# Cross-covariance attention with a highway layer: small loads moved to SyncE's queue, one more chunk of norms off TensorE, loads kept away from DMA transposes

## The chip, the cores and the metric

The kernel runs on one core of a Trainium2 chip. The core has TensorE (PE, matrix products), VectorE (DVE), ScalarE (ACT), GpSimd (POOL) and SyncE (SP), which work side by side and wait for each other by semaphores, and 16 DMA engines that carry out the transfers which any of them issues. The metric is the device time of one execution in microseconds; before the change the median of three runs was 268.25 us (268.19 to 269.06). The profile is of one more execution, with a span of 267.1 us from the first instruction of the program to the last.

## The reference, cut to what matters

```python
# attention; q, k, v: (4, 6336, 256) f32, tau = 1
qn = q / (norm(q, axis=1) + 1e-6)              # norms of columns, over the 6336 rows
kn = k / (norm(k, axis=1) + 1e-6)
a  = softmax(kn.transpose(0, 2, 1) @ qn / tau)  # one 256 x 256 matrix per batch
x  = (v @ a).reshape(25344, 256)
# highway layer
H  = maximum(x @ w_h, 0)
T  = sigmoid(x @ w_t + b_t)
out = T * H + (1 - T) * x                       # (25344, 256) f32
```

All of q and k of a batch has to be summed up before the first row of that batch's output can be computed.

## The kernel before, in words

*Tiling.* A batch has 6336 rows: 48 rows on each of 128 partitions, in six chunks of eight (0.5 MB each as f16, 1 MB read as f32), and a rest of 192 rows (96 partitions by 2, chunk 6). There are 25 pairs of rows a batch; pairs are numbered through, `g` from 0 to 99, so batch 3 is 75 to 99.

*Stage 1* (`stage1`, line 360) has 50 steps a batch, `s0.0` to `s3.49`. One step adds k^T q to two PSUM banks (line 372) and, for the norms, k^T k (line 374) and q^T q (line 376), of which only the diagonals are used. For the first `OFF[nm][b]` chunks (line 26: five of q in batches 1 to 3) the sums of squares are made elsewhere: ACT squares half a chunk (line 397, `sqq`), GpSimd adds it to an accumulator (line 403, `adq`), then folds it (`fsq`), and one product adds it over the partitions. The products of line 376 are left out for these chunks.

*The chain* of a batch (`plan_chain`, line 485; names `c0.` to `c3.`) takes diagonals, roots on GpSimd (line 513), scaling, exponential, transposes, the fold of the softmax with the weights of the highway layer (`fold`, line 619, which needs both weights), and leaves three 256 x 256 matrices in f16.

*Stage 2* works on pairs. v is transposed (`tr`, line 673) and moved out of PSUM (`ev`), and then come three groups of four products (line 728, names `h`, `t`, `x`), a preset of the bias by ACT or DVE (`b`, line 481 or 483), relu and gate on ACT (`r`, `g`, lines 785 and 804), and two operations on DVE (`p`, `y`, lines 815 and 861). Stage 2 of a batch is interleaved with stage 1 of the next.  For chunks 3 to 6 of batch 3 (`BY_DMA`, line 23), the transpose of v is a DMA instead (`T3.3` to `T3.6`, line 696), issued by SyncE.

*Loads and stores.* GpSimd issues all loads (`load`, line 251) as transfers that cast f32 to f16 on the way: q, k, v by chunks, and the rests of q and k of batch 0 (line 256), the weights (`load_w`, line 233, names `Lw0`, `Lw1`) and the bias row (`load_b`, line 238, `Lb0`, `Lb1`). In batch 0 the steps run over chunks 0 to 2, then the rest, then chunks 3 to 5 (`order_of`, line 350). SyncE issues stores (`O`, line 870), holds (`H`, line 904: tiny transfers that read a row of a later output buffer, and so keep the stores behind them on the queue until that chunk has been begun) and the DMA transposes, strictly in order.

*The order of all work* is the text `ORDER` (lines 36 to 112), written out by hand or by a planner outside the kernel: `Plan.run` (line 147) goes through it and emits each task; each engine executes its own tasks in that order. `/ACT` or `/DVE` after a name chooses the engine. Buffers are rings: q and k have five chunks each, v five, output chunks seven; a load waits until the users of the chunk five loads earlier are done.

Of the kernel before, what the change touches and what calls it, by code (L numbers as in the profile page):

```python
# [15 lines left out]
P = 128  # L16
# [9 lines left out]
OFF = {"q": (0, 5, 5, 5), "k": (0, 0, 0, 0)}  # L26
# [10 lines left out]
Lk0.0 Lk0.1 Lq0.0 Lk0.6 const Lq0.1 Lk0.2 Lq0.2 Lb1 Lq0.6 Lb0 Lq0.3 s0.0 Lk0.3 s0.1 s0.2 s0.3 Lq0.4.0 s0.4  # L37
s0.5 s0.6 s0.7 s0.8 Lq0.4.4 s0.9 s0.10 s0.11 s0.12 s0.13 Lk0.4.0 s0.14 s0.15 Lk0.4.4 s0.16 Lk0.5.0 s0.17
Lq0.5.0 s0.18 s0.19 s0.20 Lk0.5.4 s0.21 spt s0.22 ball s0.23 s0.48 s0.49 Lq0.5.4 s0.24 s0.25 s0.26 Lk0.5.6
s0.27 s0.28 s0.29 Lq0.5.6 s0.30 s0.31 Lk1.0.0 s0.32 s0.33 s0.34 Lq1.0.0 s0.35 s0.36 s0.37 Lw1 s0.38 spd1 s0.39  # L40
Lw0 s0.40 s0.41 Lv0.0 s0.42 Lq1.0.4 s0.43 s0.44 s0.45 s0.46 s0.47 spd0 c0.dq0 c0.g0/ACT b0/ACT c0.dq1 c0.dk0
c0.nq c0.dk1 sqq1.0.0 s1.0 c0.nk c0.iq c0.b c0.g1/ACT Lk1.0.4 c0.ik s1.1 Lv0.1 s1.2 c0.s0 s1.3 Lq1.1 c0.s1
c0.e0 Lk1.1 c0.e1 c0.tr0 c0.r0 Lv0.2 c0.v0/ACT c0.tr1 c0.r1 Lq1.2 c0.f0 c0.v1/ACT c0.a0 Lk1.2 tr0 c0.h0/DVE
c0.f1 ev0/ACT c0.t0/ACT tr2 c0.t1/DVE c0.a1 t0 ev2/ACT c0.h1/ACT tr1 g0 h0 ev1/DVE b1/DVE tr3 r0 h1 ev3/ACT t1
r1 x0 g1 s1.4 p0 tr5 b2/ACT x1 ev5/DVE sqq1.0.1 t2 y0 s1.5 p1 s1.6 g2 adq1.0.1 h2 b3/ACT y1 tr4 s1.7 r2 t3
ev4/DVE h3 g3 tr6 x2 r3 Lv0.3 b4/DVE ev6/ACT Lq1.3 p2 sqq1.1.0 s1.8 s1.9 y2 t4 adq1.1.0 x3 g4 s1.10 p3 tr7
b5/ACT s1.11 ev7/DVE s1.12 sqq1.1.1 t5 y3 h4 Lk1.3 g5 h5 Lk1.4 r4 tr8 s1.13 Lq1.4 b6/ACT ev8/DVE x4 Lv0.4 r5
tr9 t6 p4 Lk1.6 ev9/ACT s1.14 g6 tr10 y4 s1.15 b7/ACT x5 h6 ev10/ACT p5 Lq1.5 t7 r6 s1.16 adq1.1.1 y5 g7 tr11
x6 ev11/DVE b8/ACT h7 p6 s1.17 r7 t8 y6 s1.18 g8 s1.19 h8 sqq1.2.0 b9/DVE tr12 x7 ev12/DVE r8 s1.20 adq1.2.0
p7 t9 sqq1.2.1 s1.21 y7 tr14 x8 g9 s1.22 p8 b10/ACT h9 adq1.2.1 s1.23 ev14/ACT y8 r9 t10 s1.24 g10 tr15 s1.25  # L50
sqq1.3.0 b11/DVE s1.26 h10 t11 ev15/ACT adq1.3.0 s1.27 g11 x9 tr13 b12/ACT s1.28 p9 s1.29 r10 ev13/DVE s1.30
t12 y9 Lq1.6 x10 Lk1.5 g12 h11 p10 Lv0.5 s1.31 r11 s1.32 Lq2.0 y10 s1.33 b13/ACT Lk2.0 x11 sqq1.3.1 t13 Lv1.0
p11 s1.34 g13 h12 adq1.3.1 y11 tr17 r12 s1.35 ev17/DVE s1.36 sqq1.4.0 b14/DVE x12 h13 p12 tr16 t14 adq1.4.0
ev16/ACT y12 s1.37 r13 s1.38 g14 x13 sqq1.4.1 h14 b15/DVE tr18 s1.39 p13 Lq2.1 r14 t15 Lq2.2 y13 x14 g15
adq1.4.1 s1.40 b16/DVE h15 s1.41 ev18/DVE r15 p14 t16 s1.42 g16 y14 x15 Lv0.6 tr20 b17/ACT s1.43 Lk2.1 p15 t17
Lv1.3 ev20/DVE h16 y15 fsq1.0 g17 s1.44 r16 h17 b18/DVE tr21 r17 x16 fsq1.1 ev21/DVE t18 p16 tr19 x17 g18
ev19/DVE s1.45 y16 b19/ACT s1.46 p17 t19 s1.47 y17 g19 s1.48 sqq2.0.0 b20/DVE s1.49 tr22 c1.dq0 h18 ev22/ACT
c1.dk1 h19 c1.g1/ACT c1.dk0 r18 opq1 c1.dq1 r19 t20 kpq1 c1.rq c1.g0/ACT x18 c1.nq g20 tr23 s2.0 p18 ev23/ACT
Lv1.1 x19 b21/ACT c1.iq tr25 Lk2.2 s2.1 y18 ev25/ACT t21 Lv1.2 sqq2.0.1 s2.2 p19 c1.nk tr26 h20 g21 ev26/DVE
adq2.0.1 s2.3 y19 r20 s2.4 tr27 b22/ACT c1.ik x20 sqq2.1.0 ev27/DVE h21 p20 tr24 t22 r21 ev24/DVE adq2.1.0  # L60
s2.5 y20 g22 tr28 x21 ev28/ACT H5 h22 b23/ACT p21 O0.0.0 s2.6 r22 c1.b y21 sqq2.1.1 s2.7 Lq2.3 x22 c1.s0 Lk2.3
h23 c1.s1 c1.e0 p22 t23 adq2.1.1 c1.e1 c1.tr0 c1.r0 s2.8 r23 s2.9 c1.r1 g23 c1.tr1 x23 c1.v0/DVE b24/ACT y22
s2.10 s2.11 Lq2.6 c1.v1/ACT p23 t24 sqq2.2.0 Lk2.4 tr29 c1.f1 y23 Lq2.4 s2.12 c1.h1/DVE c1.t1/ACT Lv1.4 c1.f0
g24 ev29/DVE h24 adq2.2.0 c1.t0/ACT b25/DVE s2.13 r24 s2.14 t25 c1.h0/ACT c1.a1 x24 c1.a0 h25 g25 p24 s2.15
r25 s2.16 y24 s2.17 sqq2.2.1 tr30 b26/DVE x25 h26 adq2.2.1 p25 t26 r26 s2.18 y25 g26 s2.19 x26 ev30/DVE
b27/ACT H6 h27 p26 O0.1.0 t27 r27 tr32 O0.2.0 y26 s2.20 g27 x27 O0.3.0 ev32/DVE b28/ACT h28 p27 tr31 r28 t28
ev31/DVE s2.21 y27 g28 tr33 s2.22 ev33/ACT b29/DVE x28 sqq2.3.0 h29 p28 t29 r29 adq2.3.0 s2.23 y28 s2.24 g29
x29 b30/ACT h30 p29 tr34 r30 t30 y29 s2.25 Lq2.5 g30 x30 Lv1.5 sqq2.3.1 h31 b31/DVE Lk2.5 s2.26 p30 s2.27 r31
adq2.3.1 t31 ev34/DVE s2.28 y30 g31 tr35 x31 ev35/DVE b32/ACT h32 p31 tr36 r32 t32 Lq3.0 y31 s2.29 g32 Lv1.6
x32 ev36/ACT h33 p32 b33/ACT tr37 s2.30 r33 ev37/DVE t33 y32 x33 g33 tr38 h34 ev38/DVE b34/ACT s2.31 p33 r34  # L70
tr40 t34 ev40/ACT y33 s2.32 g34 tr39 x34 H8 ev39/DVE b35/ACT h35 H7 p34 tr41 r35 t35 y34 s2.33 g35 x35
ev41/DVE sqq2.4.0 h36 b36/DVE tr42 s2.34 p35 ev42/ACT t36 adq2.4.0 r36 tr43 y35 s2.35 g36 x36 sqq2.4.1 b37/DVE
h37 s2.36 p36 t37 r37 Lk2.6 ev43/DVE s2.37 g37 y36 Lk3.0 s2.38 x37 adq2.4.1 b38/ACT h39 p37 tr44 r39 t38
ev44/DVE s2.39 y37 g38 tr45 x39 ev45/ACT b39/DVE h38 Lv2.0 tr46 fsq2.0 r38 t39 s2.40 g39 x38 fsq2.1 s2.41 p39
b40/ACT s2.42 ev46/ACT Lk3.1 y39 t40 Lq3.1 tr47 p38 h40 g40 Lq3.3 s2.43 y38 r40 Lv2.1 s2.44 sqq3.0.0 ev47/DVE
x40 b41/DVE h41 p40 tr48 r41 t41 s2.45 y40 g41 x41 ev48/DVE h42 b42/ACT p41 tr49 r42 t42 y41 s2.46 g42 s2.47
H10 ev49/ACT b43/DVE h43 sqq3.0.1 O0.4.0 x42 t43 O0.6 r43 p42 tr50 s2.48 g43 y42 s2.49 ev50/ACT x43 b44/ACT
c2.dq0 tr51 c2.g1/ACT c2.dk0 t44 c2.g0/ACT c2.dq1 h44 ev51/ACT c2.dk1 g44 opq2 p43 c2.nk b45/ACT s3.0 kpq2
s3.1 c2.rq r44 y43 t45 c2.nq tr53 s3.2 g45 Lk3.2 ev53/DVE x44 c2.ik Lq3.2 b46/ACT h45 c2.iq Lv2.2 tr52 t46 p44
ev52/ACT Lk3.3 s3.3 r45 c2.b Lk3.4 y44 g46 s3.4 Lq3.4 x45 b47/ACT c2.s0 adq3.0.1 s3.5 c2.s1 c2.e0 t47 p45  # L80
c2.e1 c2.tr0 c2.r0 s3.6 g47 c2.tr1 s3.7 c2.v0/ACT c2.v1/DVE s3.8 b48/ACT y45 c2.f0 Lv2.3 s3.9 H11 c2.h0/DVE
c2.t0/ACT c2.f1 c2.r1 O0.5.0 h46 Lq3.5 c2.h1/DVE s3.10 O1.0.0 r46 t48 O1.1.0 c2.t1/ACT tr54 x46 ev54/ACT h47
g48 p46 s3.11 r47 Lk3.5 tr55 b49/DVE s3.12 c2.a0 x47 y46 ev55/ACT t49 sqq3.1.0 p47 h48 s3.13 r48 adq3.1.0 y47
s3.14 tr56 g49 x48 ev56/ACT h49 b50/DVE s3.15 p48 r49 t50 c2.a1 s3.16 Lv2.4 y48 g50 x49 s3.17 b51/ACT p49 h50
# [1032 lines left out]
```

## Time and profile before

| what | before |
|---|---|
| time, median of 3 | 268.25 us |
| span of the profile | 267.1 us |
| TensorE / ACT / DVE / GpSimd busy | 91% / 74% / 69% / 48% |
| first product of stage 1 | 11.5 us |
| DMA moved (f16 counted where f16 is written) | 67.2 MB; HBM read 78.4 MB, written 26.0 MB |
| products of line 376 in the trace (128 partitions) | 144, 217 ns long each, start to start 0.055 us |
| squares of half a chunk on ACT, line 397 | 27, 1056 ns each |
| additions on GpSimd, line 403 | 27, 2371 ns each |

Matrix products are pipelined: one of 256 columns is 272 ns long, but the next starts 0.11 us after it, so a sum of lengths overstates TensorE's work. A line with a wait reads: engine and line that waited, for whom, microseconds in total, times, longest. GB/s counts what is written, so a stretch of loads (f32 read, f16 written) that keeps all DMA engines busy shows some 210 GB/s and a stretch of stores some 400.

### The profile page before, as it was taken

The page shows a single profiled execution, that of the slowest core. Times are in us where ns is not written, and L with a number is a line of the kernel's source. Part 1 is how long each engine was busy: PE and PEld are TensorE (multiplying, and loading weights), DVE is VectorE, ACT ScalarE, POOL GpSimd, SP SyncE. Part 2 cuts the span into 40 slices and gives each one's busy share as a digit, 9 for nine tenths or more (in the row PEclk, how much of TensorE's full clock was granted, in tenths as well). Part 3 has the DMA queues.
Part 4 walks back from the last instruction along what each step waited for, and adds up shares of the span by engine and source line. Part 5 has one row for each costly group of instructions (what it writes and reads, how often), then busy time and mean ns, then how long its engine had stood idle before and what let it go on. Part 6 is the DMA issues. An engine that isn't in the chain of part 4 may idle for free.

```text
span 267.1 us, 6250 instructions
## 1 busy us (share of the span) xinstructions
PE 243.9 (91%) x2438; PEld 216.4 (81%) x2438; DVE 183.4 (69%) x380; ACT 198.7 (74%) x378; POOL 127.4 (48%) x143
## 2 busy tenths in 40 slices
PE   0298988999999999999999999999999999999980
PEld 0297975899999998899999988999989888888870
DVE  1000034768588888788879776976878889999990
ACT  1000038999796898898988978889979999999970
POOL 7324464577999299537194283517877010000000
PEclk9999999999999999999999999999999999999997
DMA  6999999999999999999999999999999999999995
GB/s 107 212 210 210 209 209 212 213 215 212 217 211 212 211 214 271 233 270 312 286 211 216 244 270 258 315 297 214 279 348 309 316 312 303 213 291 235 354 411 222
DMA packets 24413, 67.22 MB, mean 252 GB/s; under 512 B 8896, under 2 KB 11072, under 8 KB 21440
## 3 DMA queue, kind: packets, MB, share of 16 engines
q0 software_dynamic: 13472, 39.20, 74.7%
q1 hardware_dynamic: 10912, 27.63, 29.3%
q8 instruction: 19, 0.31, 0.4%
q14 instruction: 10, 0.08, 0.1%
HBM read 78.38 MB, written 25.95 MB: 391 GB/s over the span
## 4 chain that ended last, share of the span: by engine, by line
PE 77%; DMA 13%; DVE 4%; POOL 2%; issue 1%; ACT 1%; DVEq 0%; POOLq 0%
PE h L728 15%; PE t L728 15%; PE d L728 15%; PE sg L372 13%; DMA k<-in_k_dram 9%; PE sg L374 7%; PE vtps L688 6%; DMA q<-in_q_dram 3%; PE sg L376 2%; DVE pp L815 2%; PE t L768 1%; DVE o L861 1%; PE vtps L682 1%; POOL k L261 1%; PE eps L610 1%
## 5 line engine op out<-in xcount | busy, mean ns | idle before, releaser
L728 PEld LDWEIGHTS <-vtsb 128*128 128x128 f16 (+1 forms) x1044 | 98.8, 99 | 13.7 <-issue 1.3
L372 PE MATMUL sg<-q,k 128*128 128x256 f16 x384 | 83.7, 274 | 13.9 <-DMA q<-in_q_dram 12.6
L815 DVE SCALAR_TENSOR_TENSOR pp<-uu,d 128x512 f32<-128x512 f32 (+1 forms) x100 | 68.3, 683 | 20.2 <-PE d L728 15.0
L403 POOL TENSOR_TENSOR acc_q<-acc_q,sq_q 128x1024 f32<-128x1024 f32 x27 | 64.0, 2371 | 36.2 <-ACT sq_q L397 35.7
L374 PE MATMUL sg<-k 128*128 128x128 f16 x384 | 76.8, 221 | 0.0
L861 DVE SCALAR_TENSOR_TENSOR o<-h,pp 128x512 f32<-128x512 f32 x96 | 66.1, 688 | 2.8 <-DMA out_dram<-o 0.5
L804 ACT ACTIVATE uu<-t 128x512 f32<-128x512 f32 (+1 forms) x100 | 59.6, 597 | 9.4 <-PE t L728 6.4
L785 ACT ACTIVATE d<-h 128x512 f32<-128x512 f32 (+1 forms) x100 | 58.5, 587 | 9.4 <-PE h L728 7.5
L728 PE MATMUL t<-mr,vtsb 128*128 128x256 f16 (+1 forms) x348 | 52.2, 272 | 0.0
L728 PE MATMUL d<-mr,vtsb 128*128 128x256 f16 (+1 forms) x348 | 52.1, 272 | 0.0
L728 PE MATMUL h<-mr,vtsb 128*128 128x256 f16 (+1 forms) x348 | 51.5, 273 | 0.6 <-ACT mr L634 0.6
L372 PEld LDWEIGHTS <-k 128*128 128x128 f16 x384 | 37.8, 98 | 11.5 <-DMA k<-in_k_dram 8.7
L374 PEld LDWEIGHTS <-k 128*128 128x128 f16 x384 | 37.7, 98 | 7.6 <-issue 6.0
L481 ACT COPY t<-bias_all 128x512 f32<-128x512 f32 (+1 forms) x57 | 33.7, 592 | 1.1
L376 PE MATMUL sg<-q 128*128 128x128 f16 x144 | 31.9, 221 | 0.0
L397 ACT ACTIVATE sq_q<-q 128x1024 f32<-128x1024 f16 x27 | 28.5, 1056 | 0.0
L688 PE MATMUL vtps<-ident,v 128*128 128x128 f32 x144 | 27.9, 276 | 0.2
L498 DVE SCALAR_TENSOR_TENSOR junk<-sg,ident 128x128 f32<-128x128 f32 x16 | 4.6, 290 | 33.5 <-PE sg L376 32.2
L261 POOL DMA_DIRECT2D v<-in_v_dram x24 | 13.4, 559 | 21.9 <-PE vtps L682 13.3
L483 DVE COPY t<-bias_all 128x512 f32<-128x512 f32 (+1 forms) x26 | 18.0, 692 | 6.4 <-ACT uu L804 5.8
L483 DVE COPY vtsb<-vtps 128x256 f32<-128x256 f32 (+2 forms) x45 | 18.8, 418 | 4.8 <-PE vtps L688 4.6
L261 POOL DMA_DIRECT2D q<-in_q_dram x28 | 15.4, 550 | 11.8 <-DMA q<-in_q_dram 4.5
(77 smaller groups left out, 222.1 us busy)
## 6 DMA issues: line engine op xcount, KB each, us to landing
out_dram<-o SPq DMA_DIRECT2D x23, 1024.0 KB, 19.4
v<-in_v_dram POOLq DMA_DIRECT2D x24, 512.0 KB, 15.6
k<-in_k_dram POOLq DMA_DIRECT2D x21, 512.0 KB, 13.2
q<-in_q_dram POOLq DMA_DIRECT2D x21, 512.0 KB, 13.9
q<-in_q_dram POOLq DMA_DIRECT2D x5, 256.0 KB, 11.2
k<-in_k_dram POOLq DMA_DIRECT2D x5, 256.0 KB, 9.9
out_dram<-o SPq DMA_DIRECT2D x2, 512.0 KB
out_dram<-ot SPq DMA_DIRECT2D x4, 192.0 KB, 6.1
```

Source lines behind the costliest of these rows:

```text
L372: nc.tensor.matmul(sg[c][:, 0:C], kc, qa, start=first, stop=False)
L374: nc.tensor.matmul(sg[c][:, C : C + P], kc, kc, start=False, stop=False)
L376: nc.tensor.matmul(sg[c][:, C + P : C + 2 * P], qa[:, cs], qa[:, cs], start=False, stop=last)
L403: eng.tensor_tensor(out=acc, in0=acc, in1=sq_t.pop((nm, b, j, n)), op=AluOp.add)
L481: nc.scalar.copy(out=out, in_=in_)
L483: nc.vector.tensor_copy(out=out, in_=in_)
L688: nc.tensor.transpose(ps[:, u, 0:nr], v.bitcast(f32), ident0[0:nr, 0:nr])
L728: nc.tensor.matmul(out[0:nr, u, :], vt[u][kt][:, 0:nr], mr[kt][:, col * C : (col + 1) * C], **flags(u, kt))
L785: nc.scalar.activation(out=d[0:nr, :, :], in_=h[0:nr, :, :], func=Act.Relu, scale=scale)
L804: nc.scalar.activation(out=uu[0:nr, :, :], in_=ps_t.pop(("t", b, i))[0:nr, :, :], func=func, scale=scale)
L815: nc.vector.scalar_tensor_tensor(out=pp[0:nr, :, :], in0=el.pop(("uu", b, i))[0:nr, :, :], scalar=1.0, in1=d[0:nr, :, :], op0=AluOp.add, o ...
L861: nc.vector.scalar_tensor_tensor(out=ot, in0=ps_t.pop(("h", b, i))[0:nr, :, :], scalar=0.0, in1=el.pop(("pp", b, i))[0:nr, :, :], op0=AluO ...
```

## The change

Three things are changed, and the text of the order is a new one.

1. Weights, bias and the rests of batch 0 come as f32 through SyncE's queue, at the very start, into buffers that stage 2 uses later (`uu`, `pp`), and ACT or DVE cast them to f16 (`kb`, `kq0.6`, `kk0.6`, `kw0`, `kw1`). It is meant to use a queue that is idle then, and to take the work of issuing them from GpSimd.
2. The norms of a sixth chunk of q of batch 3 are taken off TensorE.
3. The new order lets no load of v run beside a DMA transpose: the loads of batch 3's v come in another order, and the transposes follow each other with one store and two holds between them.

```diff
-OFF = {"q": (0, 5, 5, 5), "k": (0, 0, 0, 0)}
+OFF = {'q': (0, 5, 5, 6), 'k': (0, 0, 0, 0)}
...
-Lk0.0 Lk0.1 Lq0.0 Lk0.6 const Lq0.1 Lk0.2 Lq0.2 Lb1 Lq0.6 Lb0 Lq0.3 s0.0 Lk0.3 s0.1 s0.2 s0.3 Lq0.4.0 s0.4
+Lk0.0 Lb Lq0.0 Lw0 Lq0.1 Lq0.6 Lk0.1 Lk0.6 Lq0.2 Lw1 Lk0.2 Lq0.3 Lk0.3 const Lq0.4.0 kb/ACT Lk0.4.0 s0.0
+kq0.6/DVE s0.1 s0.2 kk0.6/ACT s0.3 s0.4 s0.5 Lk0.4.4 spt s0.6 ball spd1 s0.7 b0/ACT kw0/ACT kw1/ACT Lq0.4.4
...
-    def load_w(w, m):
-        nc.gpsimd.dma_start(
-            out=wht[:, :, m * C : (m + 1) * C], in_=w.rearrange("(jl kt) m -> jl kt m", kt=2)
-        )
-
-    def load_b(u):
-        nc.gpsimd.dma_start(out=btb[0:1, u, :], in_=moe_b_t.rearrange("(a m) -> a m", a=1))
+    brow = const.tile([1, C], f32, tag="brow")
+    staged = {}
+
+    def load_w(w, m):
+        staged["w", m] = st = new("uu", [P, 2, C], f32, f"w{m}")
+        nc.sync.dma_start(out=st, in_=w.rearrange("(jl kt) m -> jl kt m", kt=2))
+
+    def cast_w(m, e):
+        copy(e, wht[:, :, m * C : (m + 1) * C], staged.pop(("w", m)))
+
+    def load_b():
+        nc.sync.dma_start(out=brow, in_=moe_b_t.rearrange("(a m) -> a m", a=1))
+
+    def cast_b(e):
+        for u in range(2):
+            copy(e, btb[0:1, u, :], brow)
...
+    def load_rest(nm):
+        staged[nm] = st = new("pp", [P, 2, C], f32, f"{nm}_rest")
+        nc.sync.dma_start(out=st[0:TR, :, :], in_=tail_rows(src_of[nm][0]))
+
+    def cast_rest(nm, e):
+        tiles[(nm, 0, NJ)] = t = new(f"tail_{nm}", [P, 2, C], f16, f"{nm}0_t")
+        copy(e, t[0:TR, :, :], staged.pop(nm)[0:TR, :, :])
```

What the new order does on the queues of SyncE and GpSimd, name by name (before, after):

```
GpSimd, start   before  k0.0 k0.1 q0.0 k0.6 const q0.1 k0.2 q0.2 b q0.6 b q0.3 k0.3 q0.4.0 ...
                after   k0.0 q0.0 q0.1 k0.1 q0.2 k0.2 q0.3 k0.3 const q0.4.0 ...
SyncE, start    before  nothing before the first hold
                after   b w0 q0.6 k0.6 w1
GpSimd, v       before  v2.5 v3.1 v2.6 v3.0 v3.3 v3.4 v3.2 v3.6 v3.5
                after   v2.5 (sums of the norms of batch 3) v2.6 v3.0 v3.3 v3.4 v3.6 v3.2 v3.1 v3.5
SyncE, end      before  O2.6 H17 T3.3 T3.4 H16 O2.4 O2.5 T3.5 T3.6 O3.0 O3.1 O3.3 O3.2 O3.4 O3.5.0 O3.5.4 O3.6
                after   O2.6 T3.3 O2.2 H15 T3.6 H16 T3.4 T3.5 O3.0 O3.2 O2.5 O3.1 O3.3 O3.4 O3.5.0 O3.5.4 O3.6
```

## The prediction

> **What bounds the kernel now.** I read the page first (busy shares, forty slices, chain), then what the matrix engine waits for, then stretches of the span, then the queue of the stores.
>
> ```profile
> PE 243.9 (91%) x2438; PEld 216.4 (81%) x2438; DVE 183.4 (69%) x380; ACT 198.7 (74%) x378; POOL 127.4 (48%) x143
> PE   0298988999999999999999999999999999999980
> DMA  6999999999999999999999999999999999999995
> PE 77%; DMA 13%; DVE 4%; POOL 2%; issue 1%; ACT 1%; DVEq 0%; POOLq 0%
> ```
>
> Two resources are full from end to end: TensorE works in every slice but the first and the last, and the DMA engines are busy in all forty. TensorE owns 77% of the chain; the transfers own the head. The list of what TensorE waits for says the same in times:
>
> ```profile
> PE sg L372 <- DMA q<-in_q_dram: 12.6, 2, 11.5
> PE sg L372 <- DMA k<-in_k_dram: 1.1, 1, 1.1
> PE h L728 <- ACT mr L634: 0.6, 2, 0.3
> ```
>
> 11.5 us until the first chunk of q is there, 1.1 us at 25.8 us for the fourth chunk of k, 1.1 us at 38.4 us for q of batch 1; after 52.2 us it hardly waits at all. The stretches show the two ends:
>
> ```profile
> 0.00:3.00 3.00, 0.00 (x0) 0.00 (x0) 0.00 (x0) 1.28 (x1) 1.97 (x8) 1.00 0.21 15
> 11.50:37.00 25.50, 24.33 (x303) 22.22 (x302) 0.14 (x1) 0.58 (x1) 9.94 (x18) 1.00 1.11 209
> 237.00:243.00 6.00, 6.00 (x56) 5.19 (x54) 5.76 (x10) 5.18 (x11) 0.00 (x0) 1.00 0.97 355
> 243.00:248.00 5.00, 5.00 (x47) 4.28 (x45) 4.66 (x8) 4.76 (x10) 0.00 (x0) 1.00 1.16 132
> 248.00:261.00 13.00, 11.38 (x101) 9.73 (x98) 12.29 (x19) 10.25 (x20) 0.00 (x0) 1.00 0.99 403
> 261.00:267.10 6.10, 0.00 (x0) 0.00 (x0) 0.12 (x1) 0.00 (x0) 0.00 (x0) 0.69 0.55 208
> ```
>
> (Stretch, its length, busy time of PE, PE's loads, DVE, ACT, POOL, clock, DMA share, GB/s.) From 243 to 248 us the DMA engines are "busy" (1.16) and move 132 GB/s, a third of what they move before and after: those are transposes of v. Then they run at 403 GB/s until after the last compute at 261. SyncE's queue explains it:
>
> ```profile
> 225.54 10.26 SPq L696 DMA_TRANSPOSE vT<-v  x2
> 236.58 0.90 SPq L875 DMA_DIRECT2D out_dram<-o  x2
> 237.59 8.09 SPq L696 DMA_TRANSPOSE vT<-v  x1
> 245.78 1.20 SPq L696 DMA_TRANSPOSE vT_t<-v_t  x1
> 247.07 13.10 SPq L875 DMA_DIRECT2D out_dram<-o  x7
> 261.15 0.33 SPq L873 DMA_DIRECT2D out_dram<-ot  x1
> ```
>
> The stores of batch 3 leave only at 247, seven in 13 us, and the last one (192 KB) took 4.9 us to land by the list of transfers, because it stood behind a backlog. So the end of the span is set by stores, the middle by TensorE, the start by loads.
>
> **What the Trainium skill says.** "DMA: Bandwidth & Descriptors", section "Queues, rings and completion order": each DMA engine takes turns between queues, packet by packet. The trace agrees: from 104 to 107 us loads and stores had 50% and 51% of the engines. Same page, section "SWDGE vs HWDGE vs iDMA": a transfer that casts has to come from GpSimd; so the moved loads arrive as f32 and need a cast on another engine, as the diff has it. Same page, "Specifications": first byte after about 0.6 us for SyncE's kind of issue, 1 us for GpSimd's. The first load here is issued at 1.24 and its first packet is seen at 2.6, so 1.4 us; no run yet shows SyncE's at the start. "Advanced Engine Details and Errata", section "X-Bar Transpose (TRN2)": transposes are as fast as other DMAs. This trace differs: issues of 4.1, 6.0 and 8.1 us for 512 KB, where a 512 KB load (1 MB read) lands every 2.45 us.
>
> **The change part by part.**
>
> *Head.* Before, SyncE issues nothing until 98.9 us. After, it issues the bias row, both rests (192 KB each) and both weights (256 KB each) at once, 0.9 MB, beside GpSimd's loads, whose order becomes k0, q0, q1, k1 where it was k0, k1, q0. Chunks land 2.45 us apart: before 6.5 (k0), 9.0 (k1), 11.4 (q0). q0 as second would land at 9.0; the 0.9 MB at 428 GB/s (1.05 MB in 2.45 us) is 2.1 us. If none of it comes first TensorE starts at 9.0, if all does, at 11.1. SyncE's packets are small (2 KB rows against 8 KB read per packet) so turn by turn they get less than half: I take 10.0, a start 1.4 us earlier.
>
> This is not 1.4 us of gain. Batch 0 then waits for its loads. After the fourth chunk of k TensorE did 24 steps of 0.443 us plus two bias spreads of 0.22 and ended at 36.9; the last chunk had landed at 35.9, so compute ran only 1 us behind the transfers. Bytes before that last chunk: the weights join (0.52 MB, +1.2 us; before, they came after batch 0, issued at 32.3 and 33.6), the two cast bias loads, which landed 0.2 us apart each, go (−0.4), and SyncE may fill part of the empty 3 us at the start (−0.3 to −0.8). Sum 0 to +0.5: stage 1 of batch 0 ends at about 37.2, +0.3. After that the weights no longer stand in the line, so k of batch 1, on which TensorE waited until 52.2 (0.26 us), is 0.7 us earlier: −0.3. Net 0, bounds −0.9 (if SyncE's loads run wholly in the empty start) and +0.9 (if not at all, and the chain pays).
>
> *Casts.* Six instructions: bias twice 256 wide (an ACT copy of 256 took 0.38 us), two rests, two weights (512 wide, 0.59 on ACT, 0.69 on DVE): 0.8 + 0.6 + 0.7 + 1.2 = 3.3 us, in a stretch where ACT was busy 0.58 and DVE 0.14 of 25.5 us. Who waits for them: the bias spread, two steps of 48 and 49 (about 21 us) and the fold at 42 us; all land near 12. I take nothing. GpSimd loses five issues of 0.5 to 0.7 us; nothing.
>
> *Sixth chunk of q, batch 3.* OFF of q goes from 5 to 6: 8 steps x 2 = 16 products of line 376 go. Start to start they cost 0.055 us (0.22 is their length, overlapped): −0.88 us, in a stage (190 to 203 us) where TensorE has no gap. Added: two squares on ACT (1.06 each, 2.1) and two adds on GpSimd (2.37 each, 4.7). GpSimd was busy 11.3 of these 13 us, but 2.7 of it are five issues of v loads that the new order puts after the sums, and from 170 to 190 it was busy only 10.2 of 20, so earlier adds can move up. The column norms of q wait for the last add and the folding; queued behind on GpSimd are the power for the norms and the loads of v. ACT was busy 10.8 of 13 us, and the new order gives DVE three of its bias copies (−1.8). If this shift fails ACT adds up to 1 us. I take −0.88.
>
> *No load beside a transpose.* Loads of v of batch 3 come in another order (chunk 1 goes last but one instead of first; chunk 5, the last, is freed by chunk 0 instead of chunk 1), and on SyncE's queue one store and two holds stand between the four transposes; the store of chunk 5 of batch 2 moves behind two stores of batch 3. Before, chunk 5's transpose was issued at 237.6 and had to wait until 243 for 2 MB of stores ahead of it. Transposes that meet nothing move at about 287 GB/s at their best, 1.8 us for 0.5 MB. The first stores of batch 3 would go at about 240, not 247: 5 us of backlog less, more than the 1.7 that there was. The last store then costs what an unhindered one does: the first load lands 5.27 us after its issue, 2.45 of it transfer, so 2.8 us fixed, and 0.46 for 192 KB: 3.3 instead of 4.9, −1.65. Bounds: 0 (backlog stays) and −2.0 (3.2 us, what the small transpose took, and less behind the half chunk ahead of it).
>
> Sum: 0 − 0.88 − 1.65 = −2.5 us: 268.25 − 2.5 = 265.75, said as 265.8.
>
> **The rivals.**
> 1. *The end stays store-bound, 267.3.* The new order puts the store of chunk 5 of batch 2 behind that of chunk 2 of batch 3, which has to be computed first (about 243), and the queue is in order, so stores could bunch again. For it: seven stores in 13 us filled the queue before. Against: 4 MB need 9.9 us, and over 20 us remain from 240. Only −0.9 is left.
> 2. *All is given back, 268.2.* A chunk of v or the later start of batch 1's chain costs about what the products save. For it: the chunk v1 is now issued only when chunk 5 of batch 2 has been transposed (about 215.6), and a load issued at that time before took 13.9 us, while its first user ran at about 225. Against: that load shared the engines with stores, which the new order keeps back there.
> 3. *Slower, 269.8.* That load does come at 229.5 as then, TensorE waits about 3 us there, and −0.88 and part of the tail are kept: +1.5.
>
> **How the numbers follow.** Forecast 0.56, rival 1 0.17, rival 2 0.13, rival 3 0.14. The range: with the head at −0.9 and tail at −2.0 the sum is −3.8 (264.4), a little more allowed for waits that a new order also removes: 263.9. On the other side rival 2 is inside and rival 3 by half: 269.0. 0.3% is 0.8 us: faster below 267.45, slower above 269.05. Forecast and most of rival 1 (0.14) are faster: 0.70; the rest of 1 and 2 the same: 0.16; rival 3 slower: 0.14.
>
> **What would show it.** Right: TensorE's first wait near 10 us, longer waits for loads up to 26, end of batch 0's stage near 37; 144 products of line 376 become 128; no wait of TensorE on v between 218 and 232; stores of batch 3 from about 240; the last store landing in 3.3 us; DMA idle in part of the last 10 us. Wrong: a wait of the v transposes on a load near 225, stage 1 of batch 0 ending past 38, or the final store again over 4.5 us after its issue.

## The result, and the profile after

The changed kernel takes 271.21 us (median of four runs, 270.84 to 272.48) where the kernel before takes 268.22 (four runs, 267.83 to 269.06): a ratio of 1.0116 with a 95% interval of 1.0073 to 1.0158. It is 3.0 us slower, not 2.5 us faster. The spans of the two profiles differ by 2.6 us (269.8 and 267.1).

The page of the changed kernel, busy shares and slices. Compared with before, TensorE has 16 instructions fewer and is busy 0.9 us less; its early hollows (slices 4, 6 and 7: 20 to 27 and 34 to 47 us) are a tenth deeper, and there is a new one in slices 16 and 17 (101 to 115 us), where before it was full.

```profile
PE 243.0 (90%) x2422; PEld 215.9 (80%) x2422; DVE 187.0 (69%) x386; ACT 200.6 (74%) x380; POOL 128.2 (48%) x139
PE   0497977999999998699999999999999999999990
PE 69%; DMA 19%; POOL 4%; DVE 3%; issue 2%; ACT 2%; POOLq 0%; DVEq 0%
```

The first line is busy time by engine, the second TensorE in forty slices of the span (6.7 us each, in tenths), the third the chain that ended last. In that chain, the transfers' share went from 13% to 19% and TensorE's from 77% to 69%. What TensorE waited for, in the changed kernel (engine, line, for whom: total, times, longest):

```profile
PE sg L410 <- DMA q<-in_q_dram: 12.1, 3, 10.5
PE vtps L720 <- DMA v<-in_v_dram: 3.2, 1, 3.2
PE sg L410 <- DMA k<-in_k_dram: 2.2, 2, 1.3
PE eps L642 <- ACT e L607: 0.8, 1, 0.8
```

The start is 1.0 us earlier (10.5 for 11.5), but there are more waits for q and k after it, one more in the chain of batch 0 (L642), and one entirely new wait of 3.2 us for a chunk of v. It ends at 110.0 us: chunk 1 of v of batch 1. GpSimd's timeline before it (start, length, instruction; in brackets the idle time ahead and who ended it) shows how it came so late:

```profile
82.88 0.56 POOL L277 DMA_DIRECT2D k<-in_k_dram  x1
85.58 2.36 POOL L441 TENSOR_TENSOR acc_q<-acc_q,sq_q 128x1024 f32<-128x1024 f32 x1 [2.13 <-ACT sq_q L435]
88.02 1.28 POOL L446 TENSOR_TENSOR acc_q<-acc_q 128x512 f32<-128x512 f32 x1
89.23 0.56 POOL L277 DMA_DIRECT2D q<-in_q_dram  x1
89.78 0.52 POOL L272 DMA_DIRECT2D v_t<-in_v_dram  x1
90.32 0.74 POOL L449 TENSOR_TENSOR sums_q<-acc_q 128x256 f32<-128x256 f32 x1
90.99 1.10 POOL L277 DMA_DIRECT2D k<-in_k_dram  x2
94.17 0.71 POOL L545 TENSOR_TENSOR inv<-x,half 128x2 f32<-128x2 f32 x1 [2.08 <-DVE junk L530]
94.84 0.57 POOL L277 DMA_DIRECT2D q<-in_q_dram  x1
95.41 0.55 POOL L277 DMA_DIRECT2D v<-in_v_dram  x1
```

From 82.9 to 89.2 us GpSimd issues no load: it waits 2.1 us for a square of ACT's, adds, and folds, with the loads queued behind. Chunk 1 of v is issued at 95.41, behind five loads that had waited too and a root for the norms (L545) that waits 2.1 us for VectorE, and lands at 109.83 by the list of transfers, 14.4 us later. Before, it was issued at 93.06 and landed at 102.82.

A pause by itself need do no harm. The kernel before has a longer one at the same place, 8.1 us from 85.0 to 93.1, and the loads write 214 GB/s all through it (last column of the second view):

```profile
79.92 1.10 POOL L261 DMA_DIRECT2D q<-in_q_dram  x2
...
83.86 0.55 POOL L261 DMA_DIRECT2D k<-in_k_dram  x1
84.41 0.55 POOL L261 DMA_DIRECT2D v<-in_v_dram  x1
84.95 1.31 POOL L408 TENSOR_TENSOR acc_q<-acc_q 128x512 f32<-128x512 f32 x1
...
93.06 0.60 POOL L261 DMA_DIRECT2D v<-in_v_dram  x1
```

```profile
85.00:93.00 8.00, 8.00 (x88) 7.42 (x87) 6.59 (x20) 6.39 (x13) 2.60 (x3) 1.00 1.06 214
```

What differs is what was issued ahead of it. Before, five loads go out between 79.9 and 85.0 us, and the last of them lands at 100.36, 7.3 us after issuing resumes. In the changed kernel a single load (k2.0) goes out between 77.3 and 89.2 us. It lands at 91.83, 2.6 us after issuing resumes, and the next whole chunk only at 96.53, 4.7 us behind it, where whole chunks land 2.45 us apart in a full stream. The stretch after the pause, in the changed kernel (columns as in the prediction; last the DMA share and GB/s):

```profile
90.00:96.00 6.00, 6.00 (x66) 5.49 (x65) 5.15 (x17) 5.06 (x11) 3.91 (x8) 1.00 1.02 172
```

and in the kernel before:

```profile
90.00:96.00 6.00, 6.00 (x63) 5.45 (x61) 4.69 (x19) 5.89 (x13) 3.50 (x6) 1.00 1.08 212
```

172 GB/s written for 212: the queue of loads ran dry. 40 GB/s over 6 us are 0.24 MB as f16, about half a chunk or 1.1 us of a transfer stream that has no reserve; by the gap between the two landings the hole is 2.2 us. (Over these 6 us the share of busy engines hides it, 1.02 for 1.08; only from 91 to 92 us does it fall, to 0.75. The bytes tell.)

The end, in the timeline of SyncE's queue in the changed kernel:

```profile
227.82 8.84 SPq L728 DMA_TRANSPOSE vT<-v  x1
236.72 0.56 SPq L907 DMA_DIRECT2D out_dram<-o  x1
237.34 0.68 SPq L938 DMA_DIRECT2D held_row<-o  x1
238.12 1.98 SPq L728 DMA_TRANSPOSE vT_t<-v_t  x1
240.15 0.66 SPq L938 DMA_DIRECT2D held_row<-o  x1
240.91 5.53 SPq L728 DMA_TRANSPOSE vT<-v  x2
246.54 16.70 SPq L907 DMA_DIRECT2D out_dram<-o  x8
264.22 0.33 SPq L905 DMA_DIRECT2D out_dram<-ot  x1
```

The first store of batch 3 leaves at 246.54 (the prediction had 240; before it was 247.07), because the first transpose took 8.8 us: 3 MB of stores had been issued just ahead of it (220 to 222 us), and chunk 5 of v, issued at 225.92, landed only at 236.82 beside it. From the last store's issue to the end of the span there are 5.6 us, before 6.0.

How the loss grows, read from the start of the same operation (`y`, line 893, before the change line 861, once a pair) in both traces: 1.2 us behind at pair 0, 1.0 at pair 16 (89 us), 4.7 at pair 24 (114 us), 3.7 at pair 48, 2.9 at pair 64, 3.1 at pair 99. Since the interleaving of the two batches differs, values within a batch are good to some half a microsecond; the last one is what counts.

### The profile page after: what moved, and what is told of

Same layout as the page of the kernel before. It is cut to its first block, busy times and chain, and to the rows that moved or that the text cites. A ratio compares the mean times of both kernels' runs of the same rounds, so it can differ in the third digit from the quotient of the medians.

```text
span 269.8 us, 6237 instructions
## 1 busy us (share of the span) xinstructions
PE 243.0 (90%) x2422; PEld 215.9 (80%) x2422; DVE 187.0 (69%) x386; ACT 200.6 (74%) x380; POOL 128.2 (48%) x139
## 4 chain that ended last, share of the span: by engine, by line
PE 69%; DMA 19%; POOL 4%; DVE 3%; issue 2%; ACT 2%; POOLq 0%; DVEq 0%
PE h L760 14%; PE d L760 14%; PE t L760 14%; PE sg L410 10%; DMA q<-in_q_dram 8%; PE vtps L720 6%; DMA v<-in_v_dram 5%; DMA k<-in_k_dram 5%; PE sg L412 5%; DVE pp L847 2%; PE t L800 1%; PE ah L654 1%; PE vtps L714 1%; POOL acc_q L441 1%; POOL k L277 1%
## 5 line engine op out<-in xcount | busy, mean ns | idle before, releaser
L441 POOL TENSOR_TENSOR acc_q<-acc_q,sq_q 128x1024 f32<-128x1024 f32 x29 | 68.6, 2366 | 41.7 <-ACT sq_q L435 41.3
L760 PE MATMUL t<-mr,vtsb 128*128 128x256 f16 (+1 forms) x348 | 52.2, 272 | 0.0
L435 ACT ACTIVATE sq_q<-q 128x1024 f32<-128x1024 f16 x29 | 30.6, 1055 | 0.2 <-DMA q<-in_q_dram 0.2
L236 ACT COPY t<-bias_all 128x512 f32<-128x512 f32 (+1 forms) x50 | 29.5, 590 | 0.9
L414 PE MATMUL sg<-q 128*128 128x128 f16 x128 | 28.3, 221 | 0.0
L238 DVE COPY t<-bias_all 128x512 f32<-128x512 f32 (+1 forms) x33 | 22.8, 692 | 7.3 <-ACT uu L836 6.4
L277 POOL DMA_DIRECT2D k<-in_k_dram x28 | 15.4, 551 | 18.5 <-DMA q<-in_q_dram 9.1
L236 ACT COPY vtsb<-vtps 128x256 f32<-128x256 f32 (+2 forms) x49 | 19.7, 402 | 6.0 <-PE vtps L720 5.7
## 6 DMA issues: line engine op xcount, KB each, us to landing
out_dram<-o SPq DMA_DIRECT2D x23, 1024.0 KB, 11.5
```

Of the source, the lines that this page charges most:

```text
L236: nc.scalar.copy(out=out, in_=in_)
L277: nc.gpsimd.dma_start(out=t[:, s : s + n, :], in_=main_rows(src)[:, j * CH + s : j * CH + s + n, :])
L435: nc.scalar.activation(out=out, in_=x, func=Act.Square)
L441: eng.tensor_tensor(out=acc, in0=acc, in1=sq_t.pop((nm, b, j, n)), op=AluOp.add)
L760: nc.tensor.matmul(out[0:nr, u, :], vt[u][kt][:, 0:nr], mr[kt][:, col * C : (col + 1) * C], **flags(u, kt))
```

## The experiments

Lags below are those of pair 99 behind the kernel before, unless another pair is named. A lag is read from one profiled execution each, and these lie off the medians: 268.91 us for the kernel before (0.7 above), 272.08 in experiment 1 (1.5 above), 277.15 in 2 (1.7 above), 270.02 in 3 (0.7 above), 272.15 in 4 (1.3 above) and 268.77 in 14 (0.8 below). In the others the distance is at most 0.4 us, experiment 12 apart. What an edit is worth is taken from the medians; a lag says where the time goes. "ORDER" is the text that orders all work.

**1. Chunk 1 of v earlier by one load.**

```diff
 in ORDER, of the changed kernel: the two loads change places
-... Lq2.3 ... Lv1.1 ...
+... Lv1.1 ... Lq2.3 ...
```

> The changed kernel with two loads of GpSimd exchanged: chunk 1 of v of batch 1 (v1.1) takes the place of chunk 3 of q of batch 2, which takes v1.1's. Theory (one late load, v1.1, is the loss): TensorE's wait of 3.2 us for v near 110 us goes, 271.2 becomes 268.0, the time of before, and the lag of about 3 us from pair 24 on shrinks to under 1 us. Rival (the wait is only a symptom of transfers that lag as a whole): another load is waited for soon after, and the time stays above 270.

Measured 270.60 (before on the same chip 268.15), ratio 1.009 [1.0061, 1.012]. The wait for v at 110 us is gone, but what TensorE waits for is now this:

```profile
PE sg L405 <- DMA q<-in_q_dram: 14.2, 4, 10.7
PE sg L405 <- DMA k<-in_k_dram: 2.6, 3, 1.1
```

q waits 2.1 us more than in the changed kernel, 1.9 of it at 142 us, k waits 0.8 us at 131, and the lag is 4.2 us by pair 40. From 90 to 96 us the loads still write only 160 GB/s. Moving the hole from one load to another doesn't fill it: the transfers as a whole were late, and this load was only the first to show it. Whether the exchange gains anything is not shown: six runs went from 269.47 to 272.08, and the interval overlaps that of the changed kernel.

**2. The same chunk of v later, in the kernel before.**

```diff
 in ORDER, of the kernel before
-... Lv1.1 x19 b21/ACT c1.iq tr25 Lk2.2 s2.1 y18 ev25/ACT t21 Lv1.2 ...
+... x19 b21/ACT c1.iq tr25 Lk2.2 s2.1 y18 ev25/ACT t21 Lv1.2 Lv1.1 ...
```

> The kernel before with one load moved back: v1.1 is issued after v1.2 instead of before k of chunk 2 of batch 2, two chunks later. Theory: it lands near 110 instead of 102.8, TensorE waits 3 to 4.5 us for it at about 106, and the time is 271 to 272.5. Rival: the wait is made good in the stages after it, under 269.5.

275.47 for 268.15, ratio 1.0259 [1.0236, 1.0282].

```profile
PE vtps L683 <- DMA v<-in_v_dram: 6.0, 1, 6.0
```

One wait of 6.0 us at 111 us, a lag of 8.1 at pair 24, and as much at the end: more than was expected, and none of it made good. The other 2 us of the lag are not waiting. Behind the wait, until 115.9 us, TensorE is granted half its clock (the third number from the end):

```profile
111.00:115.90 4.90, 4.90 (x22) 3.32 (x23) 1.51 (x3) 2.42 (x6) 0.00 (x0) 0.50 1.08 212
```

In the changed kernel the clock stays at 1.00 after its wait of 3.2 us. So a single late chunk of v is enough to cost microseconds, and what is lost at 110 us stays lost; but the size of this loss can't be set beside that of the changed kernel.

**3. The head alone, on the kernel before.**

```diff
 the kernel before, with part 1 of the change: its code, and its ORDER up to s0.47
-OFF = {'q': (0, 5, 5, 6), 'k': (0, 0, 0, 0)}
+OFF = {"q": (0, 5, 5, 5), "k": (0, 0, 0, 0)}
```

> The kernel before with part 1 alone: the changed kernel's order up to the last step of stage 1 of batch 0, with weights, bias and rests on SyncE; the order of before from there on, five chunks of norms. Theory (the head costs: 0.5 MB of weights now stand ahead of batch 0's last chunk): last chunk lands 0.7 us later, stage 1 of batch 0 ends near 37.6 instead of 36.9, and the time is 0.4 to 1.0 us above before. Rival, the prediction's: no difference, within 0.3 us.

269.30 for 268.15, ratio 1.0045 [1.0031, 1.0059]: +1.15 us. The lag is 0.76 from pair 4 to 56 and 0.49 at the end. The span of the profile is 1.1 us longer, so about half of that comes behind the last pair: from the last store's issue to the end there are 6.6 us, before 6.0. Why is not known.

**4. The sixth chunk of norms alone, on the kernel before.**

```diff
-OFF = {"q": (0, 5, 5, 5), "k": (0, 0, 0, 0)}
+OFF = {"q": (0, 5, 5, 6), "k": (0, 0, 0, 0)}
 in ORDER: the squares and additions of chunk 5 are put in after s3.43 and s3.45,
 the second square and both additions of chunk 4 move up,
 and four loads of v (v3.1 v2.6 v3.0 v3.3) move behind the fold of the sums
```

> The kernel before with part 2 alone: six chunks of q of batch 3 with norms off TensorE, the additions moved ahead of four loads of v; nothing else. Theory, the prediction's step: 16 products fewer, 0.88 us less. Rival: squares and additions end later than the products that they replace, the norms of batch 3 come later and the gain is given back: within 0.3 us of before or slower.

270.84 for 268.15, ratio 1.0102 [1.0077, 1.0126].

```profile
PE vtps L677 <- DMA v<-in_v_dram: 2.2, 1, 2.2
PE t L723 <- ACT t L476: 1.3, 1, 1.3
PE vtps L683 <- DMA v<-in_v_dram: 1.0, 1, 1.0
```

This doesn't measure the sixth chunk: a load of v that had to stand behind the added sums came 2.2 us late at 223 us, and TensorE then ran at half its granted clock (0.50 from 224.1 to 227.4 us). Pair 99 is 6.0 us behind, but the span is only 3.2 us longer: the stores at the end had slack to give (3.1 us from the last store's issue to the end, not 6.0). It shows that the additions on GpSimd and the loads behind them are one queue, in this place too. The wait of 1.0 us is in a part of the order that is as before (131 us); it shows how near the edge the loads are there.

**5. Two loads early, in the changed kernel.**

```diff
 in ORDER: k2.1 and v1.1 right behind k2.0, ahead of the additions
-... Lk2.0 s1.40 g16 y14 ...
+... Lk2.0 Lk2.1 Lv1.1 s1.40 g16 y14 ...
```

> The changed kernel with two loads, chunk 1 of k of batch 2 (k2.1) and v1.1, moved on GpSimd's queue to right after k2.0, ahead of the last additions of batch 1. Theory (transfers run full from 3 to 220 us in the kernel before; in the changed one GpSimd's queue ran dry from 90 to 96 us behind those additions, and the bytes not moved then, about 0.7 MB or 1.7 us, come back as waits wherever the next tight load is): rate from 90 to 110 us back at 420 GB/s, no wait over 1 us between 100 and 150 us, time 268.3 to 269.3. Rival (only the position of single loads counts): new waits of 1 to 3 us elsewhere, as when v1.1 alone was brought forward, 270.6 again.

269.42 for 268.12, ratio 1.0047 [1.0033, 1.0062]; the lag is 1.4 us. From 90 to 110 us loads and stores are back at some 420 GB/s (read, and f32 written, taken together; 371 and 394 in the changed kernel). After the chain of batch 0 one wait is left, 1.4 us for the rest of v of batch 0, at 100 us. Order of issue alone is worth 1.8 us.

**6. The same with part 2 undone.**

```diff
-OFF = {'q': (0, 5, 5, 6), 'k': (0, 0, 0, 0)}
+OFF = {'q': (0, 5, 5, 5), 'k': (0, 0, 0, 0)}
 in ORDER: sqq3.5.0 adq3.5.0 sqq3.5.1 adq3.5.1 are left out
```

> The same (changed kernel, k2.1 and v1.1 early) with part 2 undone: five chunks of q of batch 3 with norms off TensorE, the 16 products back, two squares and two additions gone. The prediction's step: 0.9 us slower than that kernel. Rival (the additions keep the loads of v of batch 3 back and the transfers short from 200 to 210 us): same or faster.

270.03, ratio 1.0078 [1.0059, 1.0098], so 0.6 us slower than experiment 5; by the lag (2.20 for 1.44) 0.76. The sixth chunk is worth 0.6 to 0.8 us; the two intervals just touch.

**7. The weights late again.**

```diff
 experiment 5, with the weights cast by GpSimd's loads as before
-Lk0.0 Lb Lq0.0 Lw0 Lq0.1 Lq0.6 Lk0.1 Lk0.6 Lq0.2 Lw1 ... b0/ACT kw0/ACT kw1/ACT ... Lq1.0.0 s0.36 ...
+Lk0.0 Lb Lq0.0 Lq0.1 Lq0.6 Lk0.1 Lk0.6 Lq0.2 ... b0/ACT ... Lq1.0.0 Lw1 Lw0 s0.36 ...
```

> The same (changed kernel, k2.1 and v1.1 early) with the weights loaded as before, by GpSimd as f16 after batch 0's chunks; bias and rests stay on SyncE. Theory (the 0.5 MB of weights ahead of batch 0's last chunk is the head's loss): the last chunk of batch 0 lands 1.2 us earlier, stage 1 of batch 0 ends near 36.4 instead of 37.6, 0.8 to 1.2 us faster than with the weights first. Rival (the 0.5 MB only change places, and the transfers are short later): within 0.3 us.

269.33, ratio 1.0046 [1.0031, 1.0061]: as experiment 5. The first wait falls from 10.7 to 9.8 us and the wait for q of batch 1 ends at 37.9 us instead of 39.4, but in the chain of batch 0 another takes its place:

```profile
PE eps L632 <- ACT e L597: 1.7, 1, 1.7
```

The exponential stands on ACT behind a square of q of batch 1 (`sqq1.0.1`) which the new order puts ahead of it and which itself waits for a load. The product behind that exponential starts at 42.0 us, in experiment 5 at 42.2. And something else is lost: in this profile TensorE's granted clock is 0.50 from 43.4 to 46.8 us, where it is 1.00 in experiment 5, and pair 0 comes 0.6 us later than there. So this run doesn't show what the weights' bytes cost by themselves.

**8. The tail with 4 MB of stores less.** Four stores of the kernel before (chunks 4 and 5 of batch 2, 0 and 1 of batch 3) write one partition only; the rest of these rows of the output is left out.

```diff
+            np_ = 1 if (b, j) in ((2, 4), (2, 5), (3, 0), (3, 1)) else P
             nc.sync.dma_start(
-                out=main_rows(ob)[:, j * CH + s : j * CH + s + n, :],
-                in_=og[(b, j)][:, s : s + n, :],
+                out=main_rows(ob)[0:np_, j * CH + s : j * CH + s + n, :],
+                in_=og[(b, j)][0:np_, s : s + n, :],
```

> The kernel before, leaving out most of four stores (chunks 4 and 5 of batch 2, 0 and 1 of batch 3: one partition of 128 is stored), 4 MB less in the last 30 us. If the end is set by the backlog of stores: the last store lands 3.3 us after its issue instead of 4.9, 1.65 us less, about 266.5. If it costs its 4.9 us without a backlog too: within 0.4 us of before, and the prediction's step on the tail had nothing to win.

266.00 for 268.12, ratio 0.9921 [0.9906, 0.9935]: −2.1 us. TensorE's work is unmoved, and the last store, issued at 261.27 as before, lands after 2.06 us instead of 4.94. So the backlog at the end was real, and worth 2.1 us.

**9. Three loads early.**

```diff
-... Lk2.0 s1.40 g16 y14 ...
+... Lk2.0 Lv0.6 Lk2.1 Lv1.1 s1.40 g16 y14 ...
```

> The changed kernel with the rest of v of batch 0 (v0.6), k2.1 and v1.1 right after k2.0 on GpSimd's queue. With k2.1 and v1.1 alone a wait of 1.4 us on v0.6 was left at 100 us, because these two now stood ahead of it. Theory: that wait goes too, no wait over 0.7 us between 53 and 160 us, 1.0 to 1.4 us faster than with two loads early, 268.0 to 268.4, the time of before. Rival: a further wait shows up at 107 or later and it stays near 269.4.

268.73 for 268.18, ratio 1.0017 [1.0007, 1.0027]. The waits of TensorE, and the stretch that had run dry:

```profile
PE sg L404 <- DMA q<-in_q_dram: 12.1, 3, 10.5
PE sg L404 <- DMA k<-in_k_dram: 1.2, 1, 1.2
PE eps L636 <- ACT e L601: 0.8, 1, 0.8
```

```profile
90.00:96.00 6.00, 6.00 (x66) 5.49 (x64) 5.15 (x17) 5.06 (x11) 2.87 (x5) 1.00 1.08 213
```

Three issues of half a microsecond each, moved ahead of the last addition and the fold, take back 2.5 of the 3.0 us: 213 GB/s, and no wait for v. Behind k2.0, which lands at 91.9 us, the rest of v and k2.1 follow at 92.4 and 94.9, without the hole. In the profiled execution the last pair is computed 0.25 us earlier than before the change.

**10. The square behind the exponential, on experiment 9.**

```diff
-... sqq1.0.1 s1.2 Lv0.2 s1.3 c0.s0 Lq1.2 c0.s1 c0.e0 Lk1.2 c0.e1 ...
+... s1.2 Lv0.2 s1.3 c0.s0 Lq1.2 c0.s1 c0.e0 Lk1.2 c0.e1 sqq1.0.1 ...
```

> The same (three loads early), with one square of batch 1 (second half of chunk 0 of q) moved on ACT behind the two exponentials of batch 0's chain. Theory (in the changed kernel ACT waits for that half chunk, landed at 40.4, and squares it until 41.5, with the exponential of the chain queued behind; before, the exponential started at 40.15): the chain ends 0.4 to 0.8 us earlier and the time falls by as much. Rival (the exponential would have waited for VectorE's scaling anyway): within 0.3 us.

268.99, ratio 1.0028 [1.0017, 1.0040]: a miss, no gain.

```profile
PE eps L636 <- ACT et L230: 1.2, 1, 1.2
```

The square now stands ahead of the next thing that the chain needs from ACT (the cast `et`), and the chain's two waits for ACT add up to 1.7 us, where they had been 1.3. In this profile TensorE's granted clock is 0.50 from 44.6 to 47.9 us. Six of the twelve runs, this one among them, have a mean clock of 0.984 to 0.986, and their median is 269.1; the other six have 0.99 or more and 268.75, level with experiment 9. So the runs with the higher clock show no gain either.

**11. Weights late too, on experiment 10.** The diff is that of experiment 7.

> The same (three loads early, square behind the exponentials), with the weights loaded by GpSimd after batch 0's chunks as before; bias and rests stay on SyncE. Theory (the weights' bytes ahead of batch 0 cost 1.2 us of landing, which was hidden in the earlier run by the square on ACT that waited for a half chunk landing as late as ever): now 0.8 to 1.2 us less than without, 266.5 to 267.3, faster than before. Rival: no difference again, the bytes only change places.

268.40, ratio 1.0006 [0.9996, 1.0017]: 0.6 us better than experiment 10, and level with the kernel before. Moving the weights, worth nothing in experiment 7, is worth 0.6 us here. Against experiment 9 the two moves together are worth 0.3 us, which the intervals don't separate. That the load and ACT's queue both held the chain is the likely reason, but not shown: TensorE's waits for ACT in the chain are those of experiment 10.

**12. The transposes first, on experiment 11.**

```diff
-... H17 ... O2.0.0 ... O2.4.0 ... O2.3.0 ... O2.6 ... T3.3 ... T3.4 ...
+... T3.3 T3.4 H17 ... O2.0.0 ... O2.4.0 ... O2.3.0 ... O2.6 ...
```

> The same as the one with late weights, and the DMA transposes of chunks 3 and 4 issued ahead of the four stores of batch 2 that stood before them. If transposes cost by waiting behind stores (8.8 us for the first one in the changed kernel): each takes 4 us or less, the stores of batch 3 leave 3 us or more earlier, and up to 1.5 us come off the end. Rival: beside the loads of v that still run then they take as long, the stores behind them come late for the output buffers, and the time is the same or worse.

No verdict: of six runs one took 268.26 us, level with experiment 11, and five took 279.81 to 289.71. The profile is of one of the five (283.4), in which SyncE's queue has:

```profile
214.07 22.66 SPq L718 DMA_TRANSPOSE vT<-v  x2
```

Two transposes of 512 KB held the queue for 22.7 us beside the loads of v; TensorE then waited 5.0 us for v and 7.5 for an output operation of VectorE. But the same kernel also ran in 268.26, and that run was not profiled. So it stays open whether transposes beside loads are what makes the others slow, and whether the aim of part 3 was sound.

**13. The head of before, on experiment 9.**

```diff
 experiment 9, with the kernel before's code for weights, bias and rests,
 and everything up to s1.7 in the kernel before's ORDER; parts 2 and 3 stay
```

> This kernel is e9 (the changed kernel with three loads early) with the head of the kernel before: weights, bias and rests cast by GpSimd, and all up to step s1.7 in the order of before; parts 2 and 3 stay. Theory: the head costs 0.8 to 1.15 us and the dry queue is mended, so 268.73 - 1.0 = 267.7 us, some 0.5 us under the kernel before, with y99 about 1 us ahead of before. Rival: the head's loss is made good later wherever transfers are ahead of TensorE, so nothing comes back: 268.6 to 268.8.

268.51 for 268.16, ratio 1.0009 [0.9999, 1.0019]: 0.2 us less than experiment 9. The rival was nearer: taking the head out of the mended kernel gives almost nothing, and nothing that the intervals separate, though the head alone cost the kernel before 1.15 us. There is no wait over 0.5 us after 38.4 us in its trace; but ten of TensorE's starts between 50 and 223 us come over 0.25 us after the start before them, 4.4 us in all, where the kernel before has six, 2.6 us, and experiment 9 seven, 2.5 us. Many stand where a batch's chain hands over (108, 161, 162, 217 us). That is 1.8 us of small waits against the 0.9 that the sixth chunk saves. This reading comes from the trace; no run changed these handovers.

**14. Part 3 undone, on experiment 13.**

```diff
 experiment 13, with everything behind the fold of the sums of batch 3 (fsq3.1) in the kernel before's ORDER
-Lv2.6 Lv3.0 Lv3.3 Lv3.4 Lv3.6 Lv3.2 Lv3.1 Lv3.5
+Lv3.1 Lv2.6 Lv3.0 Lv3.3 Lv3.4 Lv3.2 Lv3.6 Lv3.5      (stores, holds and transposes likewise)
```

> This is e13 with part 3 undone: from the fold of the sums of batch 3 on, everything (loads of v, stores, holds, transposes) stands in the order of before. Theory: part 3 brings about nothing, the last store stays behind a backlog in both: within 0.4 us of e13. Rival (the prediction's step): part 3 is worth 1.65 us, so this one is 1.2 to 2 us slower than e13. A third: part 3 costs something by the transposes that stand behind stores, and this one is over 0.4 us faster.

269.58, ratio 1.0057 [1.0036, 1.0079]: 1.1 us slower than experiment 13, between the two expectations.

```profile
PE vtps L677 <- DMA v<-in_v_dram: 1.5, 1, 1.5
...
PE vtps L683 <- DMA v_t<-in_v_dram: 0.5, 1, 0.5
```

But the prediction's reason for it doesn't appear in the profile. There TensorE waits 2.0 us for v at 217 and 221 us (the loads come after the longer sums, and v3.1 ahead of v2.6 and v3.0, which are wanted first), and pair 99 is 2.3 us later than in experiment 13. The span of the two profiles is nevertheless the same, 266.9 us: the backlog of stores had cleared in the meantime (the last half chunk landed 2.9 us after its issue, not 5.3). So in the profile of experiment 13 the last 2 us of the span belong to the stores, not to TensorE; and part 3's order of v's loads saves TensorE 2 us of waiting once part 2 is there. Since these two executions took the same time (268.77 and 268.70), they don't explain the 1.1 us between the medians, and what part 3 is worth at the tail by itself stays open: no order was found that changed the transposes and nothing else.

## Why the prediction was wrong

**What it got right.** The last rival (slower, 269.8) is what came in kind: a chunk of v too late, TensorE waiting about 3 us for it. That was luck as to the place: it named a load of batch 3 at 225 us, and for that one TensorE never waited; the late one is of batch 1, at 110 us. The changed kernel has 128 products of line 414 (the prediction's line 376), and experiment 6 gives 0.6 to 0.8 us for them (0.88 in the sum; of the five loads that it has behind the sums, v2.5 stayed ahead). The backlog at the end was there, and removing it is worth 2.1 us (experiment 8), as its bound of −2.0 had it.

**The step that failed: "after 52.2 us it hardly waits at all".** That is true of the kernel before, and was carried over to the changed one without an entry in the sum. The prediction treated the middle as TensorE's and looked for a late load only at 225 us, in the part of the order that the change named. The new order is new throughout. From 52 to 98 us, where the transfers of the kernel before are loads alone, they write 211 to 215 GB/s, as much as in batch 0's loads (209). So they are a second bound, level with the first, and only the order of issue keeps enough loads on their way, and the one that is wanted first ahead of the others. The new order puts five loads behind an addition that waits for ACT, with only one issued in the 12 us before, and v1.1 behind those. Cost 2.5 us by experiment 9, which moves three issues and nothing else. Experiment 2 shows in the kernel before what one late chunk does. Experiment 1, in which v1.1 comes in time and the queue is as dry (160 GB/s), still takes 270.60, so the one late load is not the whole loss. Experiment 9 mends both at once; how the 2.5 us divide between the dry queue and v1.1's place was not measured more closely.

Could it have been seen? Yes. In the order before, q2.1 and q2.2 stand ahead of the last addition of batch 1, v0.6, k2.1 and v1.3 ahead of the fold, and v1.1 ahead of k2.2 and q2.3. In the new one k2.0 alone stands between the last two additions, and v0.6, k2.1, k2.2, q2.2 and q2.3 all come behind the last one, v1.1 behind them. And the additions of line 403 show 35.7 us of waits for squares on GpSimd's queue before the change. A load behind such an addition is issued when ACT gets to it, not when the buffer is free. Those waits did no harm as long as enough loads were on their way. The chance of 0.14 for "slower" was set from one load where the whole order was a new one.

**Head: "Net 0".** It costs 1.15 us on the kernel before (experiment 3; its upper bound was +0.9). The start came 1.0 us earlier (1.4 predicted), and batch 0's stage ended at about 37.6 us (37.2 predicted, 36.9 before): the terms were mis-sized by 0.4 us each. The −0.3 that was to follow was more than used up: k of batch 1 did land earlier (chunk 1 at 49.0 us, before at 52.1), but the first half chunk of q of batch 1 landed at 39.17 us, before at 38.35, and the exponential then stood behind a square on ACT. In the changed kernel, with its dry queue mended, the head is worth less (0.2 us in experiment 13, 0.3 in 11, neither clear of the noise), so the costs of the parts don't add up exactly.

**Tail: "first stores of batch 3 at about 240", −1.65.** They went at 246.54, and the last store gained at most 0.4 us. The transposes were kept from most loads, but the first stood behind 3 MB of stores and beside the one load (v3.5) that its own order put there: it held the queue for 8.8 us where 1.8 was counted. From 228 to 230 us the engines move 420 GB/s of stores; the transpose's own small packets run mainly from 233 us on. The rival "the end stays store-bound" named the right thing for another reason.

**The sum** by measured terms: +2.5 (dry queue, 9), +1.15 (head, 3), −0.65 (norms, 6), tail about 0: +3.0, as measured. That it closes so well is partly luck: the head's 1.15 was measured in the kernel before, and in the mended kernel experiment 13 finds almost none of it.

None of the fourteen is faster than the kernel before with its outputs whole: the best, experiments 11 and 13, are level with it.

## What to carry to other kernels

When the transfers run at their full rate beside a full TensorE, both bound the kernel, and a new order of work has to be checked load by load for when it is issued against when it is wanted, in every stage, not only where the change says it is made. If the queue that issues the loads also computes, read what stands ahead of each load on it: an addition that waits for another engine delays every transfer behind it, and with no reserve that time is not made good. How long a pause in issuing may be depends on what is on its way when it begins: 8.1 us did no harm here, 6.3 us did. Look at bytes per second in short stretches; over 6 us a busy share of DMA engines near one didn't tell a full stream (1.08) from one that had run dry (1.02).

## What was not expected of the hardware

- A DMA transpose of 512 KB held SyncE's queue for 1.9 us at the least and 8.8 at the most in the changed kernel, the latter behind 3 MB of stores with one load beside; 2.9 us for the third with its stores cut away (experiment 8, 8.1 before), 4.1 for the third in experiment 14. The Trainium skill, "Advanced Engine Details and Errata", section "X-Bar Transpose (TRN2)", has transposes as fast as other DMAs. Here, where nothing else runs (237 to 238 us in the changed kernel), the transposes' packets move 290 GB/s, against some 420 for stores, and with traffic ahead the time on the queue differs by a factor of four.
- TensorE's granted clock was halved for a while behind some waits, and not behind others: to 0.50 for 4.9 us after the wait of 6.0 us in experiment 2, for 3.4 us in experiment 4, and for 3.4 us in the profiles of experiments 7, 10 and 11 (43.4 to 46.8 us in 7), where stage 2 of batch 0 begins. In the changed kernel and in experiments 5 and 9 it was 1.00 in the same places. What decides it is not shown.
- SyncE's early loads did not fill the empty start as fast as hoped. The first packet on its queue came at 1.66 us, 0.9 after the issue of the bias row. Issued at 1.16 us, the first 256 KB of weights landed at 3.94 (2.8 us), and in the first 12 us the queue had a quarter of the engines:

```profile
q0 software_dynamic: 386, 1.45, 61.4%
q1 hardware_dynamic: 512, 0.92, 24.5%
```

  (queue; packets, MB written, share of 16 engines, stretch 0 to 12 us of the changed kernel.) That agrees with the Trainium skill, "DMA: Bandwidth & Descriptors", section "Queues, rings and completion order", by which each engine takes turns packet by packet: with 2 KB packets beside packets that read 8 KB, SyncE's queue had the smaller share (21 to 25% of the engines in each 2 us from 4 to 12 us).
- Waits swap names. In experiments 1 and 7 the wait that was aimed at went away or shrank (3.2 us, 0.9 us), and others of about the same size came in its place (2.7 us, 0.9 us); in experiment 10 one of the chain's waits shrank by 0.3 us and the next grew by 0.7. A second thing (the stream of transfers, ACT's queue) was due soon after.
